# A gated convolution with two projections: blocks 2 and 3 take the order of the first two, and half of their convolution is evicted behind the next gate

## The chip, the cores and the metric

The kernel runs on one core of a Trainium2 chip. The metric is the time of one execution on the device, in microseconds (us). Times given for a kernel are medians of several executions; a profile is one execution, and its span is the time from its first to its last instruction.

## What is computed

The input x has 8 sequences of 4224 tokens with 192 features. The features form 8 heads of 24. First, each head is convolved along the sequence with 7 weights, which are a softmax over that head's 7 raw weights. On the result there follow a gate (a convolution over 5 tokens with weights of its own for each feature, then a sigmoid), a product with a 192 x 192 matrix, the product of both, and a second 192 x 192 matrix.

```python
w = exp(weight - max); w = w / sum(w)                    # per head, 7 taps
x = sum over k of w[h, k] * x_pad[:, k : k + S, h, :]    # 24 features a head
gate_pre = sum over k of conv_w[k] * xp[:, k : k + S, :] # 5 taps
gate = 1.0 / (1.0 + np.exp(-gate_pre))
val = x @ w_val
return gate * val @ w_out
```

## The kernel before

The tokens are cut into 14 groups (NJS, line 32) and the groups into 36 blocks (STEPS, line 69) of 188 to 502 tokens. Two halves of the batch lie beside each other, so a block's 192 features by two halves become a large tile of 128 partitions x 2 x m tokens (both halves of the first 128 features) and a small one of 128 x m (the other 64 features of both halves). Groups 0 to 3 have two blocks each, so blocks 2 and 3 are group 1, blocks 4 and 5 group 2, blocks 6 and 7 group 3.

**Convolution over 7.** It is a matmul of windows of x with a band matrix. A unit (conv_unit, line 296) is up to four windows: eight matmul instructions into one PSUM bank `pc`, one eviction on ScalarE to `e` (line 319), and, when a head is complete, DMAs that scatter it from `e` into x1 and x2 of its group (line 348), most of them issued on SP's queue; those of heads 5 to 7 of groups 0 to 2 are issued on GpSimd's. The loads of further x (line 159) are issued from the same place on SP. A group's units are done one or more blocks ahead of its use: the list `todo` gives block n its number of units, which is 3, 6, 3, 5, 5, 4 for blocks 0 to 5. `conv(k)` writes out the next k units.

**Gate.** For block n, gate_open (line 373) writes the first tap to a PSUM accumulator on ScalarE, gate_taps (line 384) adds taps 1 to 4 on VectorE, gate_close (line 394) applies the sigmoid on ScalarE. Index 0 is the large tile (`pa`, line 389 and 402 for taps and closing), index 1 the small one (`pb`). There is one accumulator of each kind, so gate n + 2 can be opened only when gate n + 1 is closed.

**Projections.** Each operand is split into a rounded part and a rest: the rounded part on ScalarE (lines 410 and 418), the rest on GpSimd (411 and 419). `split(n)` does it for x, `split_gated1` and `split_gated2` for the gated product. The first projection `v` of block n and the second one `o` of block n - 1 alternate on TensorE as diagonal (445), main (455), rows (468) and columns (483). The gated product is `gated(n, q)` on VectorE (line 502); it reads the bank of v, which comes free. `project` copies o out of PSUM on ScalarE (518) and stores it (521 and 523).

**PSUM.** Five banks (pool `ps`, line 121) serve v, o and the units of the convolution in turn: a block takes one for each diagonal, two for main, two for rows of o, and one for each unit. Three more hold the gate's accumulators. Which of the free banks a tile gets isn't written in the kernel.

**Order.** The schedule is manual (line 123): each engine does its instructions in the order in which the code names them. Two loops name them. The first one (line 569) runs for blocks 0 and 1. There VectorE does one tap of gate n + 1, the gated product of block n, and then the other taps; ScalarE evicts all of a block's units and then closes gate n + 1 and opens gate n + 2. The second one (line 599) runs from block 2 on. There VectorE does all four taps of the large tile of gate n + 1 ahead of the gated product; ScalarE closes that gate and opens the next ahead of the product's split, and evicts the units later; the small tile's closing and opening come last. TensorE's order is the same in both loops.

Of the kernel before, what the change touches and what calls it, by code (L numbers as in the profile page):

```python
# [17 lines left out]
NH, KW, HC, KG = 8, 7, 24, 5  # L18
# [56 lines left out]
N = len(STEPS)  # L75
# [16 lines left out]
LAG = 2  # L92
BY_POOL, EARLY, AHEAD = 3, 4, 6
WARM = 11, 5, 14

SOON = {2: (0, 2), 3: (1, 3), 4: (3, 5), 5: (5, 8)}

# [2 lines left out]
def kernel(  # L100
# [29 lines left out]
    for g, n in enumerate(NJS):  # L130
        k = PER_LOAD[n]
# [67 lines left out]
    def zeros(k):  # L199
        pw = ps.tile([128, 512], F32, tag="p", name="pw")  # L200
        for i in range(k):
            nc.tensor.matmul(pw[:M, :WIN], lhsT=zero[:, :M], rhs=zero[:, M:], start=True, stop=True)

    zeros(WARM[0])

# [90 lines left out]
    def conv_unit(u):  # L296
        g, q, ws = units[u]
        n = NJS[g]
        if u == first_unit[g]:
            x1s[g] = xp.tile([128, 2 * XB], F32, tag="x1", name=f"x1_{g}")  # L300
            x2s[g] = xp.tile([128, XC], F32, tag="x2", name=f"x2_{g}")
        if ws[0] == (0, 0):
            es[g, q] = ep.tile([M, 4 * NMAX * WIN], F32, tag="e", name=f"e_{g}_{q}")
        e = es[g, q]
        pc = ps.tile([128, 512], F32, tag="p", name=f"pc_{u}")
        for k, (hi, j) in enumerate(ws):
            h = QUADS[q][hi]
            i, at = home[g, h]
            c = (at * n + j) * M
            nc.tensor.matmul(  # L310
                pc[:M, k * WIN : (k + 1) * WIN],
                lhsT=xtiles[i][:, c : c + M],
                rhs=band[:, 4 * q + hi, :],
                start=True,
                stop=True,
            )
        a = (ws[0][0] * n + ws[0][1]) * WIN
        w = len(ws) * WIN
        nc.scalar.copy(e[:, a : a + w], pc[:M, :w])  # L319
        done = [hi for hi, j in ws if j == n - 1]  # L320
        for hi in done:
            h = QUADS[q][hi]
            i, at = home[g, h]
            last = at == len(loads[i][1]) - 1
            if last and g >= BY_POOL:
                load_x(allowed(i))
            scatter(g, h, e[:, hi * n * WIN : (hi + 1) * n * WIN])
            if last and g < BY_POOL:
                load_x(allowed(i))
# [33 lines left out]
    def views(n, k=KG - 1):  # L363
        g, o, m = STEPS[n]
        b = second(NJS[g])
        x1v = x1s[g][:, : 2 * b].rearrange("p (a t) -> p a t", a=2)
        return x1v[:, :, o + k : o + k + m], x2s[g][:, o + k : o + k + m]
# [5 lines left out]
    def gate_open(n, i):  # L373
        if n >= N:
            return
        m = STEPS[n][2]
        if i == 0:
            acc = ps_g.tile([128, 2, 512], F32, tag="pa", name=f"pa_{n}")[:, :, :m]
        else:
            acc = ps_h.tile([128, 512], F32, tag="pb", name=f"pb_{n}")[:, :m]  # L380
        accs[n, i] = acc
        nc.scalar.mul(acc, views(n, 0)[i], cwt[:, i, 0:1])  # L382

    def gate_taps(n, i, k0=1, k1=KG):
        if n >= N:
            return
        acc = accs[n, i]
        for k in range(k0, k1):
            nc.vector.scalar_tensor_tensor(  # L389
                out=acc, in0=views(n, k)[i], scalar=cwt[:, i, k : k + 1],  # L390
                in1=acc, op0=ALU.mult, op1=ALU.add,
            )

    def gate_close(n, i):
        if n >= N:
            return
        m = STEPS[n][2]
        if i == 0:
            dst = g1s[n] = gp.tile([128, 2, MB], F32, tag="g1", name=f"g1_{n}")[:, :, :m]
        else:  # L400
            dst = g2s[n] = gp.tile([128, MB], F32, tag="g2", name=f"g2_{n}")[:, :m]
        nc.scalar.activation(dst, accs.pop((n, i)), AF.Sigmoid)  # L402
# [35 lines left out]
    def diagonal(what, n):  # L438
        if not ok(n):
            return  # L440
        acc = bank(what, n, 2)
        w, _, _, h2, l2 = operands(what, n)
        r = slice(W22, W22 + 128)
        for i, (a, b) in enumerate(parts(w, h2, l2)):
            nc.tensor.matmul(acc, lhsT=a[:, r], rhs=b, start=(i == 0), stop=False)  # L445

    def main(what, n, q):
        if not ok(n):
            return
        fresh = (what, n, q) not in banks  # L450
        acc = bank(what, n, q) if fresh else banks[what, n, q]
        w, h, l, _, _ = operands(what, n)
        r = slice(W11, W11 + 128)
        for i, (a, b) in enumerate(parts(w, h, l)):
            nc.tensor.matmul(  # L455
                acc, lhsT=a[:, r], rhs=b[:, q], start=(fresh and i == 0), stop=(not fresh and i == 2)
            )
# [14 lines left out]
    def columns(what, n):  # L472
        if not ok(n):
            return
        m = STEPS[n][2]
        acc = banks[what, n, 2]
        w = w_val if what == "v" else w_out
        x = views(n)[0] if what == "v" else g1s[n]
        cuts = [m * i // 4 for i in range(5)]
        for i in range(4):  # L480
            c = slice(cuts[i], cuts[i + 1])
            for q, p in enumerate(HALVES):
                nc.tensor.matmul(  # L483
                    acc[p, c], lhsT=w.f[:, W12 : W12 + 64], rhs=x[:, q, c],
                    start=False, stop=(i == 3),
                )

    def split(n):
        if n >= N:
            return  # L490
        x1, x2 = views(n)
        if n == 0:
            xs[n, 2] = split2(sp, "x", n, x2)
        xs[n, 1] = split1(sp, "x", n, x1)
        if n > 0:
            xs[n, 2] = split2(sp, "x", n, x2)

    def gated(n, q):
        if not ok(n):
            return  # L500
        v = g1s[n][:, q] if q < 2 else g2s[n]
        nc.vector.tensor_tensor(out=v, in0=banks.pop(("v", n, q)), in1=v, op=ALU.mult)  # L502

    def split_gated1(n):
        if ok(n):
            pr[n, 1] = split1(pp, "p", n, g1s[n])

    def split_gated2(n):
        if ok(n):
            pr[n, 2] = split2(pp, "p", n, g2s[n])  # L510
# [22 lines left out]
    def conv(k):  # L533
        for _ in range(k):
            if done[0] < len(units):
                conv_unit(done[0])
                done[0] += 1

    todo = [0] * (N + 1)
    for g in range(LAG, NG):  # L540
        a, b = SOON.get(g) or (first[g - LAG], first[g - 1])
        k = first_unit[g + 1] - first_unit[g]
# [9 lines left out]
    w_out.decode()  # L552
    zeros(WARM[1])
    conv(3)
    zeros(WARM[2])
    gate_open(0, 0)
# [9 lines left out]
    gate_close(0, 1)  # L566
    gate_open(1, 1)

    for n in range(2):
        diagonal("v", n)  # L570
        split(n + 1)
        diagonal("o", n - 1)
        main("v", n, 0)
        main("v", n, 1)
        gate_taps(n + 1, 0, 1, 2)
        columns("v", n)
        gated(n, 2)
        columns("o", n - 1)
        split_gated2(n)
        project(n - 1, 2)  # L580
        rows("v", n)
        gated(n, 0)
        gated(n, 1)
        rows("o", n - 1)
        main("o", n - 1, 0)
        project(n - 1, 0)
        main("o", n - 1, 1)
        project(n - 1, 1)
        conv(1)
        split_gated1(n)  # L590
        conv(todo[n] - 1)
        gate_taps(n + 1, 0, 2, KG)
        gate_close(n + 1, 0)
        gate_open(n + 2, 0)
        gate_taps(n + 1, 1)
        gate_close(n + 1, 1)
        gate_open(n + 2, 1)

    for n in range(2, N + 1):
        diagonal("v", n)  # L600
        gate_taps(n + 1, 0, 1, 3)
        split(n + 1)
        diagonal("o", n - 1)
        main("v", n, 0)
        main("v", n, 1)
        gate_taps(n + 1, 0, 3, KG)
        columns("v", n)
        gated(n, 2)
        gate_close(n + 1, 0)
        gate_open(n + 2, 0)  # L610
        columns("o", n - 1)
        split_gated2(n)
        project(n - 1, 2)
        rows("v", n)
        gated(n, 0)
        gated(n, 1)
        rows("o", n - 1)
        split_gated1(n)
        main("o", n - 1, 0)
        gate_taps(n + 1, 1)  # L620
        project(n - 1, 0)
        main("o", n - 1, 1)
        project(n - 1, 1)
        conv(todo[n])
        gate_close(n + 1, 1)
        gate_open(n + 2, 1)
# [91 lines left out]
```

## Time and profile before

| | |
|---|---|
| executions shown | 397.56, 392.87, 394.84 us |
| median | 394.84 us |
| the profiled execution | 392.99 us |
| its span | 391.2 us |
| mean granted TensorE clock | 0.994 |
| busy: TensorE, VectorE, ScalarE, GpSimd | 376.3, 342.5, 323.7, 254.5 us |
| DMA | 82.49 MB, mean 211 GB/s |

In the profile PE is TensorE, PEld its weight loads, DVE VectorE, ACT ScalarE, POOL GpSimd, and SPq SyncE's queue, which only issues DMAs here. A row of the timeline has the start and the duration in us, the engine, the line of the kernel, the operation, what it writes and reads by the program's names, shapes, and how many were merged (x). In square brackets stands the engine's idle time just before and what ended it. A row of the chain of waits has start, duration and what was being done in the chain that ended last. A row of busy times by stretch has the stretch, its length and the busy time of each engine in it. The granted clock is the share of TensorE's full clock that the chip allowed.

### The profile page before, as it was taken

Reading aid. Unit: us, or ns where it says so; the run is one execution under the profiler, and the core shown is the slowest. Engines: PE = TensorE matmul, PEld = TensorE weight load, DVE = VectorE, ACT = ScalarE, POOL = GpSimd, SP = SyncE. Lnnn points to the kernel's source line nnn. Section 1 sums busy time; section 2 is a strip of 40 time slices with the busy share of each in tenths; the row PEclk is TensorE's granted clock in tenths of the full one; section 3 lists DMA queues with packets and bytes.
Section 4 is the critical chain, followed back from the end, with each engine's and each line's share of the span. In section 5 each row is a group of like instructions: output and inputs, shape, how many; then the busy total and the mean of one; then the engine's idle time right before and its main releaser. Section 6 shows DMA issues by size and latency. Waiting matters only on the chain.

```text
span 391.2 us, 8622 instructions
## 1 busy us (share of the span) xinstructions
PE 376.3 (96%) x3204; PEld 320.3 (82%) x3204; DVE 342.5 (88%) x424; ACT 323.7 (83%) x525; POOL 254.5 (65%) x177
## 2 busy tenths in 40 slices
PE   8889699999999999999999999999999999999895
PEld 7778589988888888888888888888888787888684
DVE  4799778888998998998999899899899999999970
ACT  7588778988888888888889988888888888887863
POOL 1889465566667665666665666766566676776771
PEclk9999989999999999999999999999999999999999
DMA  8898797799687689778868868868987644333223
GB/s 295 235 238 244 223 260 239 225 274 217 210 253 217 184 254 256 210 220 253 227 190 256 218 185 259 205 192 254 256 227 231 209 160 146 114 135 134 81 102 148
DMA packets 38209, 82.49 MB, mean 211 GB/s; under 512 B 4856, under 2 KB 17528, under 8 KB 38168
## 3 DMA queue, kind: packets, MB, share of 16 engines
q1 hardware_dynamic: 36720, 79.90, 68.6%
q0 software_dynamic: 896, 1.31, 1.5%
q10 hardware_dynamic: 552, 0.73, 0.6%
q8 instruction: 25, 0.41, 0.5%
q14 instruction: 16, 0.13, 0.1%
HBM read 29.34 MB, written 26.00 MB: 141 GB/s over the span
## 4 chain that ended last, share of the span: by engine, by line
PE 73%; DVE 12%; ACT 5%; DMA 5%; issue 3%; SPq 1%; POOL 0%; DVEq 0%; ACTq 0%
PE pc L310 20%; PE o L455 11%; PE v L455 9%; PE v L483 7%; DVE pa L389 6%; PE o L483 6%; PE v L468 6%; PE o L468 5%; PE o L445 5%; PE v L445 4%; DVE pb L389 3%; DMA x<-e 3%; DVE g L502 2%; DMA x<-xw 1%; ACT pa L382 1%
## 5 line engine op out<-in xcount | busy, mean ns | idle before, releaser
L389 DVE SCALAR_TENSOR_TENSOR pa<-x,cwt,pa 128x1004 f32<-128x1004 f32 (+5 forms) x144 | 172.9, 1201 | 8.9 <-ACT pa L382 5.1
L411 POOL TENSOR_TENSOR xl<-x,xh 128x1004 fp32r<-128x1004 f32 (+5 forms) x36 | 74.7, 2074 | 75.3 <-ACT xh L410 58.3
L310 PEld LDWEIGHTS pc<-band,x 128*120 128x120 f32 x912 | 102.6, 186 | 5.6 <-issue 1.7
L310 PE MATMUL pc<-band,x 128*120 128x122 f32 x912 | 103.8, 271 | 2.6 <-DMA x<-xw 1.9
L389 DVE SCALAR_TENSOR_TENSOR pb<-x,cwt,pb 128x502 f32<-128x502 f32 (+5 forms) x144 | 102.3, 710 | 3.8
L502 DVE TENSOR_TENSOR g<-v,g 128x502 f32<-128x502 f32 (+5 forms) x108 | 65.8, 642 | 22.2 <-PE v L468 16.6
L411 POOL TENSOR_TENSOR pl<-g,ph 128x1004 fp32r<-128x1004 f32 (+5 forms) x36 | 79.2, 2201 | 9.1 <-ACT ph L410 6.8
L402 ACT ACTIVATE g<-pa 128x1004 f32<-128x1004 f32 (+5 forms) x36 | 34.5, 958 | 42.8 <-DVE pa L389 22.8
L419 POOL TENSOR_TENSOR pl<-g,ph 128x502 fp32r<-128x502 f32 (+5 forms) x36 | 42.9, 1191 | 35.9 <-ACT ph L418 35.9
L319 ACT COPY e<-pc 120x488 f32<-120x488 f32 x114 | 59.4, 587 | 4.9 <-PE pc L310 4.7
L518 ACT COPY ot<-o 128x502 f32<-128x502 f32 (+5 forms) x108 | 55.9, 551 | 1.5 <-PE o L455 1.0
L382 ACT ACTIVATE pa<-x,cwt 128x1004 f32<-128x1004 f32 (+5 forms) x36 | 37.8, 1050 | 4.9 <-DMA x<-e 3.9
L419 POOL TENSOR_TENSOR xl<-x,xh 128x502 fp32r<-128x502 f32 (+5 forms) x36 | 41.8, 1162 | 0.0
L483 PEld LDWEIGHTS v<-x,wvf 128*64 128x64 f32 x576 | 29.1, 136 | 11.8 <-issue 11.7
L483 PE MATMUL v<-x,wvf 128*64 128x125 f32 (+4 forms) x576 | 37.2, 270 | 0.0
L410 ACT CAST ph<-g 128x1004 fp32r<-128x1004 f32 (+5 forms) x36 | 35.1, 976 | 1.5 <-DVE g L502 1.5
L483 PE MATMUL o<-g,wof 128*64 128x125 f32 (+4 forms) x576 | 35.6, 264 | 0.0
L410 ACT CAST xh<-x 128x1004 fp32r<-128x1004 f32 (+5 forms) x36 | 34.6, 962 | 0.0
L483 PEld LDWEIGHTS o<-g,wof 128*64 128x64 f32 x576 | 30.9, 136 | 0.1
L455 PE MATMUL o<-ph,woh 128*128 128x502 f32 (+5 forms) x72 | 30.8, 428 | 0.0
L455 PE MATMUL v<-xl,wvh 128*128 128x502 f32 (+5 forms) x72 | 27.1, 377 | 0.0
L455 PE MATMUL v<-xh,wvl 128*128 128x502 f32 (+5 forms) x72 | 27.1, 377 | 0.0
(75 smaller groups left out, 570.4 us busy)
## 6 DMA issues: line engine op xcount, KB each, us to landing
x<-xw SPq DMA_DIRECT2D x64, 300.0 KB
out<-ot SPq DMA_DIRECT2D x24, 753.0 KB
x<-e SPq DMA_DIRECT2D x40, 285.9 KB
x<-xw SPq DMA_DIRECT2D x20, 360.0 KB
out<-ot SPq DMA_DIRECT2D x8, 672.0 KB
x<-e SPq DMA_DIRECT2D x32, 141.6 KB
x<-e SPq DMA_DIRECT2D x25, 171.6 KB
x<-e SPq DMA_DIRECT2D x16, 94.4 KB
```

What stands on the lines that cost most here:

```text
L310: nc.tensor.matmul(pc[:M, k * WIN : (k + 1) * WIN], lhsT=xtiles[i][:, c : c + M], rhs=band[:, 4 * q + hi, :], start=True, stop=True,)
L319: nc.scalar.copy(e[:, a : a + w], pc[:M, :w])
L382: nc.scalar.mul(acc, views(n, 0)[i], cwt[:, i, 0:1])
L389: nc.vector.scalar_tensor_tensor(out=acc, in0=views(n, k)[i], scalar=cwt[:, i, k : k + 1], in1=acc, op0=ALU.mult, op1=ALU.add,)
L410: nc.scalar.copy(h, x)
L411: nc.gpsimd.tensor_tensor(out=l, in0=x, in1=h.bitcast(F32), op=ALU.subtract)
L419: nc.gpsimd.tensor_tensor(out=l, in0=x, in1=h.bitcast(F32), op=ALU.subtract)
L455: nc.tensor.matmul(acc, lhsT=a[:, r], rhs=b[:, q], start=(fresh and i == 0), stop=(not fresh and i == 2))
L468: nc.tensor.matmul(acc, lhsT=a[p, r], rhs=b[p], start=(fresh and i == 0), stop=(not fresh and i == 2))
L483: nc.tensor.matmul(acc[p, c], lhsT=w.f[:, W12 : W12 + 64], rhs=x[:, q, c], start=False, stop=(i == 3),)
L502: nc.vector.tensor_tensor(out=v, in0=banks.pop(("v", n, q)), in1=v, op=ALU.mult)
L518: nc.scalar.copy(ots[n][:, q * m : (q + 1) * m], banks.pop(("o", n, q)))
```

## The change

The first loop now runs for blocks 0 to 3 (HEAD = 4) and the second from block 4. For blocks 2 and 3 VectorE does taps 1 and 2 of the large tile of gate n + 1 ahead of the gated product, and taps 3 and 4 behind the gated products (k = 3); blocks 0 and 1 keep one tap (k = 2). In the first loop ScalarE evicts only the first `now` units of a block ahead of closing gate n + 1 and opening gate n + 2 for the large tile; the others are evicted behind these and ahead of the small tile's closing and opening. In block 0 `now` is all three units, as before; in blocks 1, 2 and 3 it is 3 of 6, 1 of 3 and 2 of 5. The matmuls of the units stay where they were among TensorE's instructions.

```diff
+HEAD = 4
...
-    for n in range(2):
+    for n in range(HEAD):
+        k = 2 if n < 2 else 3
         diagonal("v", n)
         split(n + 1)
         diagonal("o", n - 1)
         main("v", n, 0)
         main("v", n, 1)
-        gate_taps(n + 1, 0, 1, 2)
+        gate_taps(n + 1, 0, 1, k)
         columns("v", n)
         gated(n, 2)
...
         conv(1)
         split_gated1(n)
-        conv(todo[n] - 1)
-        gate_taps(n + 1, 0, 2, KG)
+        now = todo[n] if n == 0 else todo[n] // 2
+        conv(now - 1)
+        gate_taps(n + 1, 0, k, KG)
         gate_close(n + 1, 0)
         gate_open(n + 2, 0)
         gate_taps(n + 1, 1)
+        conv(todo[n] - now)
         gate_close(n + 1, 1)
         gate_open(n + 2, 1)
 
-    for n in range(2, N + 1):
+    for n in range(HEAD, N + 1):
```

## The prediction

> **What bounds the kernel now.** I read the page first, then the chain of waits, then the timeline of blocks 1 to 4 (a block is one value of n), then busy time by stretch.
>
> ```profile
> span 391.2 us, 8622 instructions
> ...
> PE 73%; DVE 12%; ACT 5%; DMA 5%; issue 3%; SPq 1%; POOL 0%; DVEq 0%; ACTq 0%
> ```
>
> TensorE sets the end for most of the span, so an early TensorE gap is worth its length, if nothing later takes it back. The stretches below are a gap in block 2, the convolution of that block, all of block 3, a piece of the middle and one of the tail. Columns: stretch, its length, busy time of PE, PEld, DVE, ACT, POOL, granted clock, DMA share, GB/s.
>
> ```profile
> 43.85:47.00 3.15, 0.00 (x1) 0.00 (x0) 3.08 (x5) 0.73 (x2) 3.10 (x2) 1.00 0.75 247
> ...
> 48.50:52.60 4.10, 4.10 (x25) 4.10 (x24) 3.96 (x6) 3.30 (x8) 3.11 (x2) 0.58 0.75 204
> 52.60:63.80 11.20, 11.20 (x104) 10.11 (x103) 9.09 (x12) 9.46 (x16) 6.55 (x5) 1.00 0.87 268
> ...
> 200.00:300.00 100.00, 100.00 (x844) 84.33 (x844) 92.32 (x104) 86.62 (x136) 64.73 (x38) 1.00 0.80 230
> 300.00:350.00 50.00, 49.53 (x396) 39.74 (x396) 48.37 (x56) 43.16 (x66) 35.01 (x21) 1.00 0.48 159
> ```
>
> In block 2 TensorE stands still for 3.15 us and then runs its convolution at a granted clock of 0.58. From block 3 on it has no gap. After 300 us VectorE is the tighter engine. The timeline of block 2 says what the gap waited for:
>
> ```profile
> 39.69 0.92 ACT L402 ACTIVATE g<-pa 128x896 f32<-128x896 f32 x1
> 40.65 1.01 ACT L382 ACTIVATE pa<-x,cwt 128x896 f32<-128x896 f32 x1
> 41.39 0.99 PE L483 MATMUL v<-x,wvf 128*64 128x112 f32 x16
> 41.69 4.73 DVE L389 SCALAR_TENSOR_TENSOR pa<-x,cwt,pa 128x896 f32<-128x896 f32 x4 [2.33 <-ACT pa L382]
> 42.84 0.47 PE L468 MATMUL v<-xh,wvh 64*128 64x448 f32 x2
> 43.56 0.29 PE L468 MATMUL o<-ph,woh 64*128 64x302 f32 x1
> 46.33 1.68 DVE L502 TENSOR_TENSOR g<-v,g 128x448 f32<-128x448 f32 x3
> 47.00 0.40 PE L468 MATMUL o<-ph,woh 64*128 64x302 f32 x1 [3.15 <-DVE g L502]
> 48.56 4.33 PE L310 MATMUL pc<-band,x 128*120 128x122 f32 x24
> ```
>
> The second matmul of rows("o", 1) needs a PSUM bank that gated(2, 2) frees. That product stands behind four taps of gate 3, the taps behind the opening of gate 3 on ScalarE, and the opening behind all six evictions of block 1's convolution: ScalarE opens at 40.65, VectorE begins at 41.69 and is through at 46.4.
>
> **What the change does, part by part.** No instruction is added or removed. The orders of TensorE, GpSimd and both issue queues stay as they are; ScalarE and VectorE are reordered in blocks 1 to 3. Block 0 keeps its order (half of its three units isn't taken).
>
> *Block 1.* Three of six evictions now follow gate_close(2, 0) and gate_open(3, 0).
>
> ```profile
> 33.07 3.53 DVE L389 SCALAR_TENSOR_TENSOR pa<-x,cwt,pa 128x896 f32<-128x896 f32 x3
> 33.99 5.20 PE L310 MATMUL pc<-band,x 128*120 128x122 f32 x48
> 35.02 0.57 ACT L319 COPY e<-pc 120x488 f32<-120x488 f32 x1 [0.43 <-PE pc L310]
> 36.09 1.19 ACT L319 COPY e<-pc 120x488 f32<-120x488 f32 x2
> 36.51 2.86 DVE L389 SCALAR_TENSOR_TENSOR pb<-x,cwt,pb 128x448 f32<-128x448 f32 x4
> 40.06 0.37 PE L455 MATMUL v<-xh,wvh 128*128 128x448 f32 x1
> ```
>
> The third eviction ends at 37.28 and the taps of gate 2 at 36.60, so the closing can start at 37.3 and, with the old step of 0.96 from closing to opening and 1.01 for the opening, gate 3 is open at 39.2 instead of 41.66. VectorE is free of its pb taps at 39.37. The three late evictions run 39.2 to 40.8; the bank of the first of them is free at about 39.8, and TensorE asks for a third bank of block 2 at 40.06. That costs nothing, by 0.3 us; an unkinder order of banks is rival 3.
>
> *Block 2.* VectorE does two taps (4.73 / 4 = 1.18 each) from 39.4 to 41.75. In block 3 the product follows the start of columns by 1.14 and the next two follow rows by 0.98 (rows below), so gated(2, 2) runs 42.5 to 43.15, before TensorE asks at 43.6. **The 3.15 us go.** With the gap I take the slow clock to go too: the chain of waits has the same 24 convolution matmuls at
>
> ```profile
> 48.72 4.17 PE pc L310 x24
> 102.56 2.52 PE pc L310 x24
> ```
>
> so **another 1.65 us.** Gross gain 4.80 us, and block 3 starts at 52.65 - 4.80 = 47.85.
>
> *What is given back.* Two taps and the rest come later now. In-order on VectorE: gated(2, 0) and (2, 1) 43.8 to 45.0, taps 3 and 4 of gate 3 to 47.35, four pb taps (2.86) to 50.2: against 50.9 before (46.33 + 1.68 + 2.86). So VectorE gains 0.7 where TensorE gains 4.8. On ScalarE a closing now waits with evictions queued behind it, and TensorE waits for the banks of these, SP for their data. I walk block 3 of before, shifted, with its own steps:
>
> ```profile
> 52.65 0.45 PE L445 MATMUL v<-xh,wvh 128*128 128x448 f32 x1
> 54.56 0.36 PE L455 MATMUL v<-xh,wvh 128*128 128x448 f32 x1
> 55.26 0.99 PE L483 MATMUL v<-x,wvf 128*64 128x112 f32 x16
> 56.40 0.62 DVE L502 TENSOR_TENSOR g<-v,g 128x448 f32<-128x448 f32 x1 [0.98 <-PE v L483]
> 56.96 0.47 PE L468 MATMUL v<-xh,wvh 64*128 64x448 f32 x2
> 57.68 0.36 PE L468 MATMUL o<-ph,woh 64*128 64x448 f32 x2
> 57.94 1.16 DVE L502 TENSOR_TENSOR g<-v,g 128x448 f32<-128x448 f32 x2 [0.92 <-PE v L468]
> 59.72 4.36 PE L310 MATMUL pc<-band,x 128*120 128x122 f32 x40
> 59.90 0.94 ACT L410 CAST ph<-g 128x896 fp32r<-128x896 f32 x1
> 61.59 1.52 ACT L319 COPY e<-pc 120x488 f32<-120x488 f32 x3
> 63.84 0.45 PE L445 MATMUL v<-xh,wvh 128*128 128x448 f32 x1
> 68.87 0.37 PE L468 MATMUL o<-ph,woh 64*128 64x448 f32 x2
> ```
>
> Block 2's convolution runs from 45.4. First eviction about 46.4 (in block 1 it followed the convolution's start by 1.03: 33.99 to 35.02), end 46.95, split of the gated product (0.94, overlapping a little with its neighbours) to 47.75, closing of gate 3 (its taps end 47.35) and opening of gate 4 to 49.7, second eviction to 50.2, third to 50.7 (three take 1.52). TensorE asks for block 3's fourth bank at 47.85 + 1.91 = 49.76: **0.5 back.** Block 3's product stands behind only two taps (50.2 to 52.55, product to 53.2) and rows("o", 2) asks at 53.4: in time. Convolution from 55.4; products 0 and 1 to 54.8, taps to 57.15, pb to 60.0. ScalarE: first eviction 56.45, split, second eviction to 58.3, closing of gate 4, opening of gate 5 59.3 to 60.3. Block 4, in the old order again, has all four taps ahead of its product: 60.3 to 65.05, product to 65.7. TensorE starts that block at 59.5 (55.4 and the 4.1 from 59.72 to 63.84) and asks at 59.5 + 5.03, plus a first matmul of 0.1: **1.05 back.** Block 4's rows then run at 65.7 instead of 68.87. Sum: 4.80 - 0.50 - 1.05 = **3.2 us**.
>
> In block 5 VectorE has two products to 66.9, pb taps to 69.7 and four taps to 74.5, while TensorE is due for the product at 65.7 + 2.04 + 4.1 + 3.75 = 75.6 (rows to convolution, convolution, start to product, all from block 3's rows): VectorE is ahead again. From there to 300 us it waited 16 us in all for TensorE:
>
> ```profile
>   DVE g L502: 16.0, 25
> ```
>
> It can follow 3.2 us, and its tail starts earlier by as much. Bounds: if ScalarE is as fast as VectorE needs, the taps of gate 5 start at 59.6, the last wait shrinks by 0.7, and the gain nears 4.0; if both waits vanish it is 4.8. From below: each wait can grow, and I price that as rivals. The moved evictions delay their scatters on SP by less than 2 us (closing 0.96 and opening 1.01). Behind them stand loads of x, which SP issues long ahead:
>
> ```profile
> 39.83 0.48 SPq L159 DMA_DIRECT2D x<-xw  x1
> ```
>
> This is the last of those that block 2's convolution reads, now wanted from 45.4, 5.6 us after the issue. An early load took 4.86 in the chain of waits:
>
> ```profile
> 14.83 4.86 DMA x<-xw
> ```
>
> So it lands in time; if late, by under 1 us, which the wait at block 4 mostly covers.
>
> [...] The granted clock was 0.58 over the 4.1 us after a gap of 3.15 us. [...]
>
> **The rivals.**
> 1. *The taps hide all.* The banks are handed out so that no late eviction is waited for, and ScalarE, whose starts follow each other closer than its busy times, opens gate 5 in time. For: in block 2 the convolution began at 48.56, before the copy that frees the diagonal's bank (48.90), so banks aren't handed out in plain rotation. Against: ScalarE is busy 9.46 of block 3's 11.2 us already. Gain 4.0 to 4.8.
>
> ```profile
> 48.90 0.40 ACT L518 COPY ot<-o 128x302 f32<-128x302 f32 x1
> ```
>
> 2. *The gap goes, the slow clock stays* in some block before 4. TensorE's 1.65 us come back, but part of it falls into the two waits above: block 3 from 49.5, its convolution from 56.6, opening of gate 5 to 61.45, taps to 66.2, rows of block 4 at 66.8 instead of 68.87. Gain 2.1.
> 3. *Slower: the first bank of a block is the last evicted.* If diagonal("v", 3) gets the bank of block 2's last unit, it waits from 47.85 to 50.7: 2.85 us, near the 3.15 that went with a slow clock, so 1.65 more. Block 3's convolution then ends at 63.5, its last eviction, behind closing 4 and opening 5, at 64.4, where block 4 started at 63.84: 0.6 slower; with a slow clock once more in block 4, 2.3 slower. It decides from the point where the waits for banks pass 4.8 us. Against: the allocator would have to hand out banks in an order in which the last is wanted first.
>
> **How the numbers follow.** The profiled execution took 392.99 us, its span of 391.2 and 1.8 around it; less 3.2 is 389.8. The median of the runs shown is 394.84, 1.85 above it, with a spread of 392.87 to 397.56; the forecast for a median is 394.84 - 3.2 = **391.6 us**. Chances: forecast 0.50 (own range 390.6 to 392.8: gains of 4.2 to 2.0), rival 1 0.22 (390.0 to 390.8), rival 2 0.15 (392.7), rival 3 0.13 (395.4 to 397.1). About 1% is what a measurement can tell from no change, so faster means below 390.9, slower above 398.8. Faster: rival 1 nearly whole, the better third of the forecast: 0.38. Slower: the far end of rival 3 and the spread of the runs, 0.08. Within: 0.54. The range goes from the fastest run shown less the gross gain (392.87 - 4.8 = 388.1) to the middle of rival 3 with some spread, 396.0.
>
> **What would show it.** Right: no wait of TensorE for a gated product in block 2, granted clock 1.0 from 44 us on, opening of gate 3 at about 38.2, block 3 starting at 47.8, a wait of about 1 us for the product of block 4 and a short one for an eviction at block 3; from block 5 on every row 3 us earlier. Wrong: a stretch at half clock in blocks 2 to 4 (rival 2), TensorE waiting for ACT e L319 by more than 2 us in all (rival 3), or no wait at block 4 (rival 1). The prediction falls if the gap in block 2 stays, or if VectorE, not TensorE, sets the pace of blocks 5 to 20.

## The result and the profile after

The change takes 391.06 us (median of 12 executions, 390.09 to 393.35) against 394.14 us before (12, 392.82 to 397.56): 0.9923 of the time, 95% interval 0.9897 to 0.995. A second set of runs on another occasion gave 390.74 against 394.97 us, 0.9898 (0.9865 to 0.9931). So 3 to 4 us, just under or about 1%.

The profiled execution is a poor witness for the total. The lines of its page:

```profile
span 391.6 us, 8620 instructions
...
PEclk9969999999999999999999999999999999999999
...
PE 72%; DVE 13%; DMA 5%; ACT 4%; issue 3%; SPq 2%; POOL 0%; DVEq 0%; ACTq 0%
```

Its span is no shorter than before (391.2). The third digit of the clock shows why. By stretch, first before, then after (columns as in the prediction):

```profile
20.00:24.00 4.00, 4.00 (x44) 3.34 (x43) 3.86 (x7) 3.07 (x6) 3.30 (x5) 1.00 0.96 229
```

```profile
20.00:24.00 4.00, 3.63 (x18) 3.66 (x19) 3.82 (x7) 0.78 (x3) 3.49 (x5) 0.50 0.99 229
```

In this execution TensorE waited 3.78 us for a load of x (timeline below) and ran at half clock from 19.36 to 26.19 us, so block 2 starts at 42.69 instead of 38.95 us.

```profile
20.37 5.21 PE L312 MATMUL pc<-band,x 128*120 128x122 f32 x24 [3.78 <-DMA x<-xw]
```

Neither lies in what the change moved: block 2 started at 40.79 in a second execution of the same kernel, and between 38.90 and 42.69 in all the profiles here. Therefore the stage is measured from the start of block 2 (its first matmul of `diagonal`) to the start of block 6. This stretch repeats within 0.02 us from one execution of a kernel to another:

| from one start to the next, us | before | after |
|---|---|---|
| block 2 (to block 3) | 13.70 | 8.50 |
| block 3 | 11.19 | 11.79 |
| block 4 | 11.17 | 12.26 |
| block 5 | 10.35 | 10.35 |
| block 2 to block 6 | 46.41 | 42.90 |
| block 2 to the end | 352.25 | 348.87 |

5.20 us come from block 2, 0.60 and 1.09 are given back in blocks 3 and 4, and nothing of size happens later (the last row repeats only within 0.4 us: 348.47 in the second execution). The timeline of after, blocks 1 and 2 (lines are two higher than before):

```profile
40.91 0.92 ACT L404 ACTIVATE g<-pa 128x896 f32<-128x896 f32 x1
41.86 1.01 ACT L384 ACTIVATE pa<-x,cwt 128x896 f32<-128x896 f32 x1
42.69 0.45 PE L447 MATMUL v<-xh,wvh 128*128 128x448 f32 x1
42.81 1.49 ACT L321 COPY e<-pc 120x488 f32<-120x488 f32 x3
43.00 2.34 DVE L391 SCALAR_TENSOR_TENSOR pa<-x,cwt,pa 128x896 f32<-128x896 f32 x2
46.26 0.62 DVE L504 TENSOR_TENSOR g<-v,g 128x448 f32<-128x448 f32 x1 [0.92 <-PE v L485]
47.30 0.31 PE L470 MATMUL o<-ph,woh 64*128 64x302 f32 x2
48.75 2.68 PE L312 MATMUL pc<-band,x 128*120 128x122 f32 x24
50.88 2.86 DVE L391 SCALAR_TENSOR_TENSOR pb<-x,cwt,pb 128x448 f32<-128x448 f32 x4
```

Gate 3 is opened ahead of the three late evictions, two taps end before block 2's columns do, VectorE now waits for TensorE (0.92) instead of the other way round, and both first matmuls of rows go together. The convolution runs at full clock (2.44 us from its start to block 3's start at 51.19; 4.09 before). By stretch, the convolution, and then the timeline of blocks 3 and 4:

```profile
48.70:51.20 2.50, 2.50 (x27) 2.50 (x25) 2.46 (x4) 2.07 (x5) 2.03 (x2) 1.00 0.62 208
...
53.60 0.47 PE L457 MATMUL v<-xh,wvh 128*128 128x448 f32 x1 [0.34 <-ACT e L321]
61.20 0.57 ACT L321 COPY e<-pc 120x488 f32<-120x488 f32 x1
61.66 0.93 ACT L404 ACTIVATE g<-pa 128x896 f32<-128x896 f32 x1
62.62 1.01 ACT L384 ACTIVATE pa<-x,cwt 128x896 f32<-128x896 f32 x1
63.66 4.73 DVE L391 SCALAR_TENSOR_TENSOR pa<-x,cwt,pa 128x896 f32<-128x896 f32 x4 [0.41 <-ACT pa L384]
68.30 1.68 DVE L504 TENSOR_TENSOR g<-v,g 128x448 f32<-128x448 f32 x3
68.97 0.47 PE L470 MATMUL o<-ph,woh 64*128 64x448 f32 x1 [0.59 <-DVE g L504]
```

Block 3's fourth bank waits for a late eviction. Block 4, the first in the old order, has all four taps of gate 5 ahead of its product. They start when gate 5 is open (62.62 + 1.01), 0.41 us after VectorE was free, and TensorE waits for the product behind them.

### The profile page after: what moved, and what is told of

Its sections match the earlier page's. It is cut to its first block, busy times and chain, and to the rows that moved or that the text cites. A ratio compares the mean times of both kernels' runs of the same rounds, so it can differ in the third digit from the quotient of the medians.

```text
span 391.6 us, 8620 instructions
## 1 busy us (share of the span) xinstructions
PE 378.0 (97%) x3204; PEld 321.6 (82%) x3204; DVE 342.3 (87%) x424; ACT 323.8 (83%) x525; POOL 254.8 (65%) x177
## 4 chain that ended last, share of the span: by engine, by line
PE 72%; DVE 13%; DMA 5%; ACT 4%; issue 3%; SPq 2%; POOL 0%; DVEq 0%; ACTq 0%
PE pc L312 20%; PE o L457 10%; PE v L457 9%; PE v L485 7%; PE v L470 6%; PE o L485 6%; DVE pa L391 6%; PE o L470 5%; PE o L447 5%; PE v L447 4%; DVE pb L391 4%; DVE g L504 3%; DMA x<-e 2%; DMA x<-xw 2%; DMA scr<-wv 1%
## 5 line engine op out<-in xcount | busy, mean ns | idle before, releaser
L485 PEld LDWEIGHTS v<-x,wvf 128*64 128x64 f32 x576 | 29.1, 136 | 11.8 <-issue 11.4
L457 PE MATMUL v<-xh,wvh 128*128 128x502 f32 (+5 forms) x72 | 27.2, 377 | 0.3 <-ACT e L321 0.3
```

The source lines that it names most:

```text
L457: nc.tensor.matmul(acc, lhsT=a[:, r], rhs=b[:, q], start=(fresh and i == 0), stop=(not fresh and i == 2))
L485: nc.tensor.matmul(acc[p, c], lhsT=w.f[:, W12 : W12 + 64], rhs=x[:, q, c], start=False, stop=(i == 3),)
```

## The experiments

Theory A was the prediction's: the gap comes from the late opening of gate 3, the slow clock from the gap, and the loss in block 4 from VectorE, which gains little while TensorE gains 5 us. The theories against it stand in each expectation. The measure is block 2 to block 6 (46.41 before, 42.90 after), and the ratio to before where it was timed.

| kernel | block 2 | block 3 | block 4 | 2 to 6 | ratio to before (95%) |
|---|---|---|---|---|---|
| e1, evictions only | 9.61 | 11.24 | 11.18 | 42.38 | 0.9878 (0.9846 to 0.991) |
| e6, the same again | 9.59 | 11.27 | 11.17 | 42.38 | 0.9893 (0.9857 to 0.9929) |
| e5, the change again | 8.49 | 11.80 | 12.24 | 42.88 | 0.9898 (0.9865 to 0.9931) |
| e2, taps only | 9.66 | 12.01 | 15.84 | 47.86 | 1.0043 (1.002 to 1.0066) |
| e8, four taps, late closing | 9.61 | 13.48 | 12.25 | 45.68 | 0.9963 (0.9937 to 0.9989) |
| e4, first loop to block 5 | 8.49 | 11.81 | 11.19 | 41.86 | 0.9907 (0.9875 to 0.9939) |
| e3, gap filled | 12.18 | 11.19 | 11.18 | 44.89 | 0.9963 (0.9935 to 0.9991) |
| e7, gap filled again | 12.18 | 11.19 | 11.18 | 44.89 | one execution |
| e9, e10, partly filled | 12.05, 12.06 | 11.25, 11.24 | 11.17, 11.18 | 44.82 | one execution each |

**One part alone: the evictions of block 1.** The second loop runs from block 2 as before.

```diff
 for n in range(2):
...
-        conv(todo[n] - 1)
+        now = todo[n] if n == 0 else todo[n] // 2
+        conv(now - 1)
         gate_taps(n + 1, 0, 2, KG)
         gate_close(n + 1, 0)
         gate_open(n + 2, 0)
         gate_taps(n + 1, 1)
+        conv(todo[n] - now)
```

> Block 1's evictions are split around the next gate, and blocks 2 and 3 keep the order of the second loop. Measured from the start of block 2 to the start of block 6 in the profile (before 46.41 us, after 42.90). Theory A (the early opening on ScalarE is what closes the gap; the two-tap order only moves VectorE's lag into block 4): gate 3 opens 2.4 us earlier, four taps end 44.1, so block 2 keeps a wait of about 1.1 us and loses the slow clock; block 3 waits about 0.5 us for its product and block 4 nothing; 42.7 to 43.1, as fast as the whole change within 0.2%. Theory B (both parts are needed): most of the gap and the slow clock stay, 45 or more, under 0.4% faster than before.

42.38 us: a little better than theory A had it, and 0.5 us better than the whole change. The timeline:

```profile
40.04 4.72 DVE L389 SCALAR_TENSOR_TENSOR pa<-x,cwt,pa 128x896 f32<-128x896 f32 x4
44.68 1.68 DVE L502 TENSOR_TENSOR g<-v,g 128x448 f32<-128x448 f32 x3
44.89 0.92 ACT L402 ACTIVATE g<-pa 128x896 f32<-128x896 f32 x1 [1.09 <-DVE pa L389]
45.35 0.41 PE L468 MATMUL o<-ph,woh 64*128 64x302 f32 x1 [0.70 <-DVE g L502]
46.28 2.85 DVE L389 SCALAR_TENSOR_TENSOR pb<-x,cwt,pb 128x448 f32<-128x448 f32 x4
49.03 4.73 DVE L389 SCALAR_TENSOR_TENSOR pa<-x,cwt,pa 128x896 f32<-128x896 f32 x4
53.67 0.62 DVE L502 TENSOR_TENSOR g<-v,g 128x448 f32<-128x448 f32 x1
```

Each DVE row begins where the one before ends: from the opening of gate 3 to the product of block 3 VectorE has no break, so with these taps in this order and gate 3 open at this time the stretch can't be shorter. TensorE keeps a short wait in block 2 and no other of size up to block 6. VectorE's small taps of gate 3 end 9.4 us after block 2's start (46.28 + 2.85 - 39.75). In the change that is 11.05 (50.88 + 2.86 - 42.69), and before 11.8 (- 38.95):

```profile
47.93 2.86 DVE L389 SCALAR_TENSOR_TENSOR pb<-x,cwt,pb 128x448 f32<-128x448 f32 x4
```

With two taps the product of block 2 comes early, but VectorE then stands idle for TensorE and runs later than in e1. The waits of VectorE from 38 to 76 us, in the change:

```profile
DVE g L504 <- PE v L470: 1.2, 2, 0.7
DVE g L504 <- PE v L485: 0.9, 1, 0.9
DVE pa L391 <- ACT pa L384: 0.4, 1, 0.4
```

The change differs from e1 in two things at once, though: the order of VectorE's taps in blocks 2 and 3, and ScalarE's order there (closing and opening behind evictions and the split, where the second loop has them first). The run with four taps below separates the two. To have e1 and the change on one chip, they ran once more together.

> The evictions alone (block 1's only), beside the whole change on one chip. Theory A: from the opening of gate 3 to the product of block 3 VectorE works without a break, so its work, not the order of its taps, sets this stretch; 42.4 us from block 2 to block 6, 0.5 us less than the change, 0.1 to 0.2% faster than it. Rival: the 0.4% between them in the first runs is something else (loads, chip), and the two are the same here within 0.1%, or the other way round.

> The change once more, beside the evictions alone on one chip. Both theories of it: the stretch from the start of block 2 to the start of block 6 takes 42.9 us again. If the late start of block 2 in its first profile (42.69 against 38.95) came from a load that landed late in that execution and not from the change, block 2 starts at 39 to 41 here.

The stage repeats (42.38 and 42.88). In whole times they stand at 390.43 and 390.74 us: the right order, but 0.3 us is within their intervals, so that the evictions alone are faster is shown for the stage, not for the total. The 0.4% between the first sets did not come again (0.9893 and 0.9898). Block 2 started at 40.79 and 38.90 us: the late start of the first profile belongs to that execution.

**The other part alone: the order of the first loop in blocks 2 and 3.** `now = todo[n]`, else the change. So it is not the tap order alone: in blocks 2 and 3 ScalarE, too, has the first loop's order, with every eviction ahead of closing.

> Blocks 2 and 3 take the order of the first loop with two taps ahead of the product, and no eviction is moved: all of a block's units are evicted ahead of closing the next gate. Theory A: block 2 starts its taps at the old time, two of them end at 44.05 and leave a wait of about 1.1 us and no slow clock, so block 3 starts about 4.1 us earlier; but gate 5 opens only behind five evictions, its four taps end near 68, and block 4 waits about 2.7 us; block 2 to block 6 about 45.5 to 46.5, within 0.3% of before, slower if the wait in block 4 brings a slow clock. Theory B (the two-tap order is what brings the gain): 43.5 or less.

Slower than before, by 1.5 us in the stage and 0.4% in time, somewhat worse than expected. Gate 5 opens behind five evictions:

```profile
64.93 4.73 DVE L391 SCALAR_TENSOR_TENSOR pa<-x,cwt,pa 128x896 f32<-128x896 f32 x4 [2.96 <-ACT pa L384]
70.24 0.47 PE L470 MATMUL o<-ph,woh 64*128 64x448 f32 x1 [2.66 <-DVE g L504]
```

```profile
71.00:73.00 2.00, 2.00 (x7) 1.49 (x5) 1.93 (x4) 2.00 (x4) 0.69 (x1) 0.50 0.69 191
```

The old gap returns in block 4 with its slow clock (second fence, by stretch). Without the early openings, this order only carries the wait two blocks on. Two taps with the second loop's order of ScalarE were not run.

**The change with four taps ahead of the product.** `k = 2 if n < 2 else KG`.

> The change with k = 5 for blocks 2 and 3: all four taps ahead of the product, as in the second loop, while ScalarE keeps the change's order (first evictions, then closing and opening). Theory A: VectorE doesn't wait within block 2 (a wait of TensorE of 0.8 to 1.1 us there, as with the evictions alone), but gate 4 is opened only behind block 2's first eviction and the split of the product, near 50.8 on the clock of before, VectorE waits some 2 us for it and block 3 waits 2 to 2.6 us for its product: 44.5 to 45.5 us from block 2 to block 6, more with a slow clock in block 3. Rival (ScalarE's order in blocks 2 and 3 is harmless, only the tap order costs): 42.4, as the evictions alone.

45.68 us, at theory A's side and a little beyond its upper end. VectorE waits only for openings, in two waits from 41 to 77 us:

```profile
DVE pa L391 <- ACT pa L384: 5.3, 2, 3.2
```

The timeline has the two (gates 4 and 5):

```profile
52.54 4.73 DVE L391 SCALAR_TENSOR_TENSOR pa<-x,cwt,pa 128x896 f32<-128x896 f32 x4 [2.11 <-ACT pa L384]
64.80 4.73 DVE L391 SCALAR_TENSOR_TENSOR pa<-x,cwt,pa 128x896 f32<-128x896 f32 x4 [3.17 <-ACT pa L384]
```

This kernel and e1 have the same orders on VectorE and TensorE; only ScalarE's order in blocks 2 and 3 differs, and it isn't harmless: evictions and the split ahead of closing cost 3.3 us. The change differs from this kernel in the taps alone, and two taps ahead of the product win back 2.8. So the change is the sum of three parts: the evictions of block 1 (46.41 to 42.38), ScalarE's order in blocks 2 and 3 (to 45.68), and the two taps (to 42.90). The second loop, which closes first, doesn't need the two taps. Block 4 shows it as well: with VectorE free 3.17 us before gate 5 opens it takes 12.25 us, as in the change, so the late opening alone is enough for the loss there.

**The first loop for more blocks.** `HEAD = 6`.

> The change with the first loop running for blocks 0 to 5. Theory A (the wait of 1.1 us in block 4 is VectorE's lag of 4.5 us, which four taps ahead of the product make visible, and which VectorE works off at about 1 to 1.8 us a block): block 4 no longer waits, nor does block 5, block 6 by 0.5 us at most: start of block 2 to start of block 7 51.4 to 51.8 (before 55.91, after 52.40), 0.15 to 0.25% faster than the change. Theory B (behind late evictions each block of this order waits for PSUM banks about 0.6 us as block 3 does): 52.5 to 53, no better than the change.

Wrong for both. Blocks 4 and 5 have no wait, as A said; block 3 has the same 0.6 and no later block has it, against B. But block 6, the first in the old order, takes 11.42 instead of 9.50 us, and block 2 to block 7 takes 53.28 us, more than the change's 52.40. By stretch, blocks 3 to 6:

```profile
48.20:60.00 11.80, 11.46 (x105) 10.04 (x104) 10.94 (x15) 10.32 (x17) 7.97 (x5) 1.00 0.88 260
60.00:71.20 11.20, 11.20 (x106) 10.04 (x104) 8.97 (x12) 9.51 (x17) 6.44 (x5) 1.00 0.88 231
71.20:81.60 10.40, 10.40 (x98) 9.24 (x96) 8.20 (x11) 8.74 (x16) 5.64 (x5) 1.00 0.93 268
81.60:93.00 11.40, 10.20 (x89) 8.44 (x88) 10.77 (x14) 9.82 (x17) 6.83 (x5) 1.00 0.90 250
```

VectorE is busy only 8.97 and 8.20 us in blocks 4 and 5: in the two-tap order it can't work ahead, because the product, for which it waits on TensorE, stands between the taps. The lag isn't worked off; it is carried to the first block of the old order. There the opening of gate 7 again comes last, by 0.38 us:

```profile
83.08 4.73 DVE L391 SCALAR_TENSOR_TENSOR pa<-x,cwt,pa 128x896 f32<-128x896 f32 x4 [0.38 <-ACT pa L384]
```

Block 6 has three units and is a short one; that it gives least cover for this reason wasn't tested. I had taken the idle time for progress.

**The slow clock.** The kernel before, with work for TensorE in the gap that adds zeros to a bank.

```diff
+                if what == "o" and n == 1 and i == 0 and p == HALVES[0]:
+                    for _ in range(15):
+                        nc.tensor.matmul(
+                            acc[:M, :WIN], lhsT=zero[:, :M], rhs=zero[:, M:], start=False, stop=False
+                        )
```

> The kernel before, with 15 matmuls of zeros (some 3.1 us) between the first and second matmul of the rows of o in block 2, which add nothing to its bank. Theory A (the slow clock behind the gap comes from the idle TensorE): the wait shrinks to under 0.5 us, the granted clock stays 1.0 in block 2, its 24 convolution matmuls take 2.5 us instead of 4.17, block 2 to block 6 44.8 instead of 46.41. Theory B (the slow stretch falls there by the phase of a grid, whatever this gap does): 4.1 us again, 46.4.

```profile
44.80:48.00 3.20, 3.20 (x30) 3.14 (x30) 3.13 (x5) 0.78 (x2) 3.11 (x2) 1.00 0.77 239
48.00:49.50 1.50, 1.50 (x13) 1.26 (x12) 1.50 (x3) 1.47 (x3) 0.00 (x0) 1.00 0.36 106
49.50:52.00 2.50, 2.50 (x26) 2.50 (x25) 2.39 (x5) 2.50 (x6) 1.59 (x2) 1.00 0.70 182
```

By stretch: the gap is full, the useful work no earlier, and the convolution runs at clock 1.0. 44.89 us, 1.5 less than before, as theory A had it (44.8); in time 0.9963. Over all executions the median of the mean granted clock is 0.995 (12 executions), against 0.989 before (23). A second execution (its name says half, but it is the same kernel):

> The kernel before, again with the gap in block 2 filled by 15 matmuls of zeros, a second execution: if the slow clock follows the idle TensorE, granted clock 1.0 in block 2 again and 44.9 us from block 2 to block 6; if the first was a chance of the grid's phase, 46.4.

The same 44.89. Two kernels with less filling, one execution each:

> The kernel before with 7 instead of 15 matmuls of zeros in the gap of block 2, about 1.5 us, so that TensorE stands still for some 1.9 us behind them. The wait of 1.23 us in block 6 (first loop for blocks 0 to 5) brought no slow clock, those of 2.66 us (taps only, block 4) and 3.15 us (before, block 2) did. If what counts is the length of standing still with a bound between these, either can come; 44.9 us from block 2 to block 6 if the clock stays at 1.0, 46.4 if it is halved. If any break in the stretch resets what counts, 44.9.

> The same with 4 matmuls of zeros, about 0.8 us, and some 2.5 us of standing still behind them: by the wait of 2.66 us that brought a slow clock, a slow clock and 46.4 us from block 2 to block 6; if the bound lies above 2.5 us, 44.9.

Both kept full clock in block 2, with waits of 1.49 and 2.12 us: the 24 matmuls of the convolution took 2.68 us in each, as in the change at clock 1.00, and 4.33 before. Their timelines:

```profile
47.58 0.40 PE L468 MATMUL o<-ph,woh 64*128 64x302 f32 x1 [1.49 <-DVE g L507]
```

```profile
49.60 0.41 PE L468 MATMUL o<-ph,woh 64*128 64x302 f32 x1 [2.12 <-DVE g L507]
```

The wait left in the second was shorter than I had reckoned (2.12 for some 2.5 us). These two give no bound on the length of a wait: half clock followed waits of 2.66 us (e2) and 3.15 us (before) and not this one of 2.12 us, but whether the length decides isn't shown. The last section has what went before half clock in the traces of before and of the change.

## Why the prediction was right, point by point

- *The gap goes.* Right. Its size was put at the 3.15 us of idle time; by starts it is 3.55 (block 2's start to its convolution: 9.61 before, 6.06 after). The idle time of the row counts from the modelled end of a lone first matmul, which otherwise runs beside its twin (after, 47.30: two in 0.31 us; before, 43.56: one in 0.29 us).
- *The slow clock goes with it, 1.65 us.* Right, 4.09 against 2.44, and shown by e3: only TensorE's idle time was taken away, and 1.5 us went. Rival 2 is out. How long a gap has to be for it isn't shown: half clock followed this one of 3.15 us and one of 2.66 us in e2, not one of 2.12 us in e10.
- *0.5 us back in block 3.* Right in place and cause (a late eviction's bank), 0.60 in size.
- *1.05 us back in block 4.* Right: 1.09, VectorE's four taps behind gate 5's opening. As in the prediction's walk (60.0 and 60.3), VectorE was free shortly before the opening, by 0.41 us. e8 shows that the opening alone is enough; VectorE's lag alone would leave about 0.7 (an estimate: 1.09 less 0.41).
- *Nothing later.* Right: block 5 takes 10.35 us in both kernels, and the change is 3.51 us ahead at block 6 and 3.38 at the end. The 0.13 between is within the scatter: from block 6 to the end it is 305.84 us before, 305.97 and 305.59 in two executions of the change. The prediction's remark that VectorE is the tighter engine after 300 us isn't what its row says (TensorE busy 49.53 of 50 us, VectorE 48.37), and nothing in the sum hangs on it.
- *The sum.* 3.2 us predicted; 3.4 in the profiles from block 2 to the end; 3.1 in the medians of the first runs and 4.2 in those of the second. The terms that missed (0.40 too small for the gap, 0.10 and 0.04 too small for what comes back) leave 0.26 together, so the sum was helped only a little by errors that cancel.
- *The step that the runs correct* is a reading, not a term: the prediction took the early opening and the two taps as two halves of the gain. The opening alone has all of it: with e1, block 2 loses 1.1 us of its gain, and blocks 3 and 4 give back 0.05 and nothing. The first loop's order in blocks 2 and 3 wins those 1.1 us in block 2 and pays 1.6 in blocks 3 and 4. By e8 it is ScalarE's order that costs (3.3 us), and the two taps make up for most of it (2.8). The prediction had each of these waits, but never asked what the stretch takes with the second loop's order left as it was.
- *Rival 1* (no wait is left) didn't happen: TensorE waited for a late eviction's bank (0.34 us), and VectorE for gate 5's opening (0.41). e1, which has neither wait, gained 4.0 us, the lower end of what this rival had. *Rival 3*: TensorE did wait for a bank behind a late eviction, by 0.34 us and never for the first bank of a block. Its mechanism wasn't seen, though e2 (1.0043 of the time before, with clock 0.50 in block 4) shows that a moved wait with a slow clock can make this kernel slower.

## What to carry to other kernels

When an engine gets far ahead at one place, ask how much earlier the next engine's whole queue ends, not only the instruction that was waited for: in the change VectorE's small taps of gate 3 ended 0.8 us earlier while TensorE won 5.2, and 1.7 of these were handed back within two blocks. First move what the engine behind the gap waits for (here the opening, ahead of evictions that nobody needs yet): that alone brought 4.0 us. Taking the product ahead of half of the taps paid (2.8 us) only where the opening itself was late. And compare stages from a mark inside the kernel when the first 25 us of an execution scatter by more than the effect.

## What the runs showed of the hardware

- In the traces of before and of the change the granted clock is 1.00 or 0.50, and its changes lie as on a grid, whole multiples of 3.413 us apart, called steps here. Before they come at 48.81, 52.22 and 390.14 us, 1 and 99 steps apart; in the change at 19.36, 26.19 and 391.42 us, 2 and 107 steps apart. So a piece of half clock lasted 3.41 us in the one and 6.83 us in the other, and the last 1.06 and 0.18 us of the spans, without work, are at 0.50 again. In e2 the piece of block 4 lasted from about 70.6 to 74.0 us (an estimate from the means by stretch: 0.91 from 69 to 71 us, 0.50 to 73, 0.74 to 75).
- TensorE's idle time within a step, and the clock in the next one. Between 6 us and the end of the span the two traces have eight steps in which TensorE was idle for 1 us or more:

| step, us | idle time of TensorE, us | clock in the next step |
|---|---|---|
| before, 14.67 to 18.09 | 1.50 | 1.00 |
| before, 41.98 to 45.39 | 1.54 | 1.00 |
| before, 45.39 to 48.81 | 1.61 | 0.50 |
| before, 366.24 to 369.66 | 1.04 | 1.00 |
| before, 386.72 to 390.14 (end of the work) | 3.34 | 0.50 |
| the change, 15.95 to 19.36 | 2.77 | 0.50 |
| the change, 19.36 to 22.78 (itself at 0.50) | 1.01 | 0.50 |
| the change, 388.00 to 391.41 (no work) | 3.41 | 0.50 |

No other step was followed by 0.50.

- The wait of 3.15 us before the change is the one in the second and third of these rows. The ends of matmuls are modelled in the profile, so 1.54 and 1.61 us don't fix an edge between them, and whether the idle time within a step or the length of a wait decides isn't shown. By length, half clock followed waits of 3.78 us (the change), 3.15 us (before) and 2.66 us (e2). It followed neither the 2.12 us of e10 nor the 2.2 us of e3 for a load of x: e3's mean granted clock of 0.998 over 391.0 us leaves at most 2.0 us at 0.50 (an estimate), less than one piece.
- Before, half clock set in 1.81 us after TensorE had begun again (47.00 to 48.81), in e2 about 0.4 us after (70.24 to 70.6), in the change 1.01 us before the wait ended (19.36 to 20.37). So the next work paid the price, in the kernel before the convolution (4.09 us against 2.44).
- The clock differs from one execution of the same kernel to another: the mean granted clock of the profiled ones is 0.992 (e1) and 0.997 (e6, the same kernel), 0.991 (the change) and 0.996 (e5, the same). Block 2 started between 38.90 and 42.69 us; in the latest of these TensorE had waited 3.78 us for a load and run at 0.50 for 6.83 us. In the two pairs of profiles of e1's kernel and of the change, most of the difference arises before the stage that the change touches: 0.85 of 0.94 us and 1.90 of 2.30 us.
